# A gated recurrence and a low-rank mixer on one core: one more chunk's scaled k and q transposed by a DMA of SyncE, inside a new written-out order

## The chip, the core and the metric

The kernel runs on one core of a Trainium2 chip. A core has a tensor engine (PE, with its weight loads, PEld), a vector engine (VectorE, DVE in the profile), a scalar engine (ScalarE, ACT), GpSimd (POOL) and SyncE (SP), which here only issues DMA transfers. Each engine works through its own instructions strictly in the order in which they were issued; semaphores make it wait for the other engines. The metric is the device time of one execution in microseconds (us), lower is better.

## What is computed

Two operators, one after the other, in float32 (the kernel computes the products in bfloat16):

```python
# q, k, v, alpha: [batch 4, heads 8, rows 768, 48]
for t in range(S):
    state = alpha[:, :, t, :, None] * state + einsum('bhd,bhe->bhde', k[:, :, t], v[:, :, t])
    y[:, :, t] = einsum('bhd,bhde->bhe', q[:, :, t], state)
x = y.transpose(0, 2, 1, 3).reshape(4, 768, 384)
# U: [768, 32], V: [32, 768], w_ch1: [384, 1536], w_ch2: [1536, 384]
h = x.transpose(0, 2, 1) @ U @ V
u = x + h.transpose(0, 2, 1)
out = u + maximum(u @ w_ch1, 0) @ w_ch2
```

## The kernel before

**Recurrence.** The 768 rows of a batch are cut into six chunks of 128, so there are 24 chunks, named here (batch, chunk). Within a chunk, everything is expressed through the running sum of ln(alpha). One chunk goes through these steps (lines of `stage_pair`, which serves batches 0 and 1, then of `stage_gla`, which serves batches 2 and 3):

- four loads of 192 KB by SyncE (alpha, k, q, v; lines 347 and 354);
- ScalarE takes the logarithm of alpha into `lt` (377, 566), and v is copied to bfloat16 as `rv` (378, 567; by the helper `copy`, which issues on ScalarE at line 288, VectorE at 290 or GpSimd at 292);
- TensorE sums `lt` over the rows (386 and the lines behind it, 573 to 575);
- ScalarE takes three kinds of exponentials of that sum: `ai` and `aa`, with the whole chunk's width, and `tot`, a narrow one (400 to 402, 583 to 586);
- k times `ai` and q times `aa` become the two halves of `rkq`, on GpSimd or VectorE (408, 594);
- `rkq` is transposed into `kqt`. Mostly TensorE does it, in two groups of four products (436, 608), each followed by an eviction from PSUM on VectorE or ScalarE (`copy` again). For the chunks that stand in the tuple `QUEUE_T`, one transposing DMA transfer of SyncE does both halves at once (447, 620). Before the change `QUEUE_T` holds the six chunks of batch 3;
- scores: products of `kqt` with itself (467, 636), masked by VectorE into `pm` (478, 646);
- the state: a product of `rkq` with `rv` (501, 659), added to the earlier state (identity products at 493, or a sum `sm` at 530 and 686) and scaled by `tot` into `st` (516, 670);
- the result y: a product of `kqt` with the earlier state (in `stage_pair` that is `f_yi`, line 540; 698), plus products of `pm` with `rv` (550, 703), copied into `xb`.

`stage_pair` handles two spans of 128 rows for half of the heads in one chunk, with even and odd rows interleaved. `stage_gla` handles one span for all eight heads. `PAIRS` makes every chunk of batches 0 and 1 paired and none of batches 2 and 3.

**Mixer.** `stage_mix` multiplies `xb` with U (718 for batch 0, 728 for the others), then with V (749), and VectorE adds x into `ub` (759). Batch 0 goes another way, through products with the identity (769 to 772). The result is transposed into `uT`: for batches 2 and 3 (`QUEUE_U`) by three transposing DMA transfers of SyncE (783). `mlp1` is the first layer, 12 groups of three products for each half of a batch (829), each followed by a maximum with zero on ScalarE or VectorE (839, 841). `mlp2` is the second layer (858), the sum with u on VectorE (864), and the stores (867, 869). The weights come in 24 transfers of 192 KB (line 320) and are converted on GpSimd or ScalarE.

**The order.** None of this is issued where it stands. The functions only add operations to a list (`Plan.add`: engines that may do it with a planner's cost, the function, what it reads and writes, a `mode` letter for the way that the product uses the array). `Plan.run` then issues them in the order of `TABLE`, a string written out by hand. Each three characters are two for the number of the operation and one for its engine (P, A, D, G or S); `SLOTS` says which of its buffers each operation takes. Costs, modes and `kind` matter for a planner only: with a table they change nothing.

```python
            op = self.ops[code(x[0]) * len(CODE) + code(x[1])]
            for b in op.bufs:
                if b.slot is None:
                    place(b)
                ready.discard(b)
            op.fn({"P": "PE", "A": "ACT", "D": "DVE", "G": "POOL", "S": "SP"}[x[2]])
```

So `TABLE` sets the place of each operation in its engine's queue, and for SyncE the order of all transfers: loads, transposing transfers and stores share one queue. Buffers: 40 for loads and stores (`io`), four `kqt`, four `rkq`, five `rv`, three each of `aa`, `ai` and `lt`, eight banks of PSUM.

Decoded, the first transfers of the old order are (a for alpha, "1:" for batch 1, otherwise batch 0; the first has position 1): a0, a1, k0, v1, a2, a3, k1, q1, v0, q0, V, a4, k3, k2, a5, q2, k4, v2, **q3** (19th), v3, 1:a2, k5, q5, 1:a0, v4, q4, v5, 1:a1, 1:k0, 1:q0, 1:v0, U. Then the rest of batch 1's loads and the weights follow, mixed.

Of the kernel before, what the change touches and what calls it, by code (L numbers as in the profile page):

```python
# [20 lines left out]
HEAEeAGVPELPAqSECGEEPHFABiSEGDDfPEiPD9GEMPENDDgPDhDGYAHGAGXADiAEfPEgDD4PGWABlSEDGEFPEHAEhDD3PGqABmSAJPAKAAGPAHAD5PD6AD7A
EUGEjPEkDEIPEJDEKDGsPEmPEPPAmSGvAGZGGbPGdAAoSGaGElPEOPAkSGcPGeDEnPEpABjSBpSBqSEQPESAERAGUGGiPEoDBrSAySGjDGkDBnSGuAAuSAwS
GtAADGEqPGfPErPEsDB1SEzPEwPE8PHzAEtPE2PAsSE0PGlGE1DExPEyDA6SE5PEuPEvAE3PE4AE9PE+DE6PE7DH1PH4AANGA2SB0SAjAA4SGhDARGAPGE-P
FBPFCAFXPA0SFYAFDPFEDFADFbPFZPFaDHaAAfGAhGFrPHHGFTPFpPFqABsSFRPFSAH2AHcPFUDHeAHdAATGHfAFcAGxDGwGGyPH3AAZAAVGFVPGgDAXGFfP
FJPFFPFGAFsDB4SFKDGzPG1AHIDFtPFgAFuDBwSB+SBuSG0DFHPFIAHKPHMAHJPFdPFeAFWDAdGHLDBtSGrGG5PG6DHCGHQPIKAG7DG2PHNPFhPHRDHODFiA
G3DAbGFjPFnPFoABxSB8SHgGIMPHSDG4DHTDALGINAFkAArGFPPFNPFODB5SIOAHiPB6SHkDB3SBySB9SBzSG8GHhGFQAH6GFLPHjPHPDGmPIPAB2SBvSAnA
HVPHWPH8PHlDFlPH5GH7PH9DG9PFMAH+AFmAHXPHZDHYACASGnPGoDGpACDSG+PHbGHpPHqDHmPHoDCFSHnDH-PAlGApAIBDCESG-AHAAIQGGHPISPIUAHuP
IRGITPIVDF1PCMSACSHrGHvPIWPIADHwPH0GICPAvAHyAHxAAxAHsDCGSCBSCLSHUGIDDFvPIFPGNPIYDIEGIGPAtAILGIZPHtDIaDIHPIJDIbDIIDAzGF2P
KwAFwPA7AA1AIXDA5GA3GIcPGOPIdPKyPK0AK1AKzAIePIfACCSF3PGPPFxPIgDGQDFyDF4DCYSKHAKJPIhPGBPK3GIiDIjPKLAKNAGCPGIPInDKKALFALHP
K2AKMAKOGIlDImDIoPIkDIqDIrDGDPIpDKbAKdPKgAKeAKiGKPGKQPIsDLaAItPGJPGEDIuDIvPIwDLcPK5PIxPGKDIyDKSAK7AI1PI-PI2ALLALKAJAALdA  # L30
AIGKIGJLPJMAB7SLJALNDB-SLIAKcGI9PJbPKfAKjDJHPCUSKkPKhAI+AJcACOSCaSI5PJVPJWDJPPJQDKmALMDI7PJIDKRPI8AKTDI3PJDPJNPJXPJYAJZP
JEDK4GKXPKYDKlPJaAJTPLvAI6DLeALiGLgALfAJdPJOAKnAI4DK6PK8DJUDJFPJGDNcAIzPI0AKxGKrPKsDKtGJeDJJPJKANePNfANhAKUPKWDKoPK9PK-D
KpDKVDKqDNgANkGF7PJfPJgACQSJRPJSANiAF8PLOPLQDLxPK+DLyAN-AJhPJiALzALAPL0DF9PLBDLCDLDPLEAO1AOBPOEAKuPKvDF+DLPPLkPJ7PLhGL1G
L3PJ8PLRALGGL5DL2PL4DLjPNjGLbGOFAOCALVPLWDLXGCISJ9PLlAODAOHGKZPKaALSPLmDLnPLTDL6PJBPJCALoDLUDJjPLqPLrDLsGO3PJkPJpPLpDLtP
LYPJqPLwAO4AORAL7DL8DL9PO5ANtAJlPOTPAEGCHSCNSOGGJ+DLZDJmDLuAL+AL-PMADOWAJ1POUAOVANvPNxACJSCKSN1GCPSOAGNzAJoSMBPMDDMEDMCD
NuGNlSOXAMFDNwANyAJ2PKBPMGPMKDMJDMHDMIDJ3PJvPOjAOlPJwPKCPJrPN0DN6PJ4DJxPJyDNdANpPMLSNqDN7DMMSOnAOMPKDPKEDN8GONDMUPMgPMQP
MhDMSPMNSMmPMnAM2PMqPMrDMRAMaPMbDJsDMOPCTSOSGMWPMVAMPAMXAMoPOoAMpAMwPOpAMsPMePMYPMZDCRSCSSOYGCWSCVSMxAOmAM8PMTAMfANmPOIS
OJPM3DOLDMyPJ5SMuPMvAMtAOKDM6PM9AMzAOPPMcPMdANIPNnDNoDNrPNsAM7DCZSO6DOZGOaSObPOdDOcDOQDN2SN3PM4PM5AOePM+PMkPOOGOhPMiPMjA
M-PMlAO7GOrGN4DN5DN9PCXSOkAOqGOfDOgGOiDOsSOtPOuDO8SO9PO-DOwPOxDNJPO+DOvDCbSO2GNXPGSSGASGGSF5SN+AM0PNAPM1AF6SGRSOyGPAPPBD
OzPO0ANBDFzSKASJzSNKPNLDPCPPDDNSPGMSPEPPHDPFDPGDPIDPOSNTPNDPPJPPNDPKDNYPPLDPMDPPSNEPNNPNUPNVDNZPNOPNFPNPPPXPPYAPfPPVPPWA  # L40
# [12 lines left out]
"""


# [103 lines left out]
def kernel(  # L159
# [205 lines left out]
    def stage_pair(b, u, sprev, xb):  # L365
# [169 lines left out]
        yb = Buf(bank), Buf(bank)  # L535

        def f_yi(e, c):
            s = before[c]
            for a in range(2):
                nc.tensor.matmul(  # L540
                    yb[c]()[:, 2 * a * D : (2 * a + 2) * D], lhsT=qcol(a, c, slice(0, 128)), rhs=s[0]()[:, 2 * s[1] + a, :],
                    start=(a == 0), stop=False, skip_group_check=True,
                )
# [379 lines left out]
```

## Time and profile before

| | |
|---|---|
| time, median of three executions | 159.53 us (159.40 to 159.62) |
| the profiled execution's own time | 159.86 us |
| its span (first to last instruction) | 158.1 us |
| mean granted TensorE clock | 0.989 |
| data moved by DMA | 31.66 MB, mean 200 GB/s |
| DMA queue 1 (all transfers of the kernel) | 95,280 packets, 84.6% of 16 engines' span |
| VectorE, longest group | masks, line 646: 24 of 682 ns and line 478: 24 of 682 ns |
| ScalarE, longest group | relu, line 839: 65 of 504 ns |
| second layer, line 858 | 300 matmuls, 53.9 us of TensorE |
| first layer, line 829 | 288 matmuls, 51.9 us of TensorE |

How to read the rows that follow. A row of the strip has 40 digits, one for each fortieth of the span (3.95 us here), and a digit is the busy share in tenths. `out<-in` names what an instruction writes and reads, and `x4` is the number of instructions. "us A, B" after a bar are the total and the mean in ns; the number behind the second bar is the idle time of that engine just before, with what ended it. Times at the left of a row are from the start of the span.

### The profile page before, as it was taken

To read this page: it belongs to the slowest core of one execution; us is meant where nothing else is said; L and a number is where in the kernel's file an instruction comes from. 1 tells how busy PE (TensorE), PEld (TensorE's weight loads), DVE (VectorE), ACT (ScalarE), POOL (GpSimd) and SP (SyncE) were. 2 spreads that over 40 slices of the span, in tenths; PEclk is the share of its full clock that TensorE was granted. 3 is DMA by queue.
4 is the path that set the end of the run, shared out by engine and by line. 5 is a ranking of instruction groups with operands and counts; after the bars stand their busy time and mean duration, and the time that the engine had idled before them with its cause. 6 is when DMAs were issued, how large, how long until landed. Compare 5 with 4: busy or idle time off the path is not lost.

```text
span 158.1 us, 4788 instructions
## 1 busy us (share of the span) xinstructions
PE 146.3 (93%) x1864; PEld 99.4 (63%) x1864; DVE 105.2 (67%) x241; ACT 86.8 (55%) x225; POOL 63.6 (40%) x104
## 2 busy tenths in 40 slices
PE   0488699999999999999999999999999999999992
PEld 0376487756677666766767775655676566556671
DVE  5089578777989647937999978463998841602621
ACT  4486669758887475595977765038642103544100
POOL 8136696493996442504546534057313000000000
PEclk9999969999999999999999999999999999999999
DMA  4999899999999998998999986799997357343172
GB/s 119 280 278 307 219 287 248 316 330 294 266 311 282 267 189 160 215 197 169 191 202 184 216 170 133 115 181 206 209 145 183 92 101 205 114 154 77 50 249 100
DMA packets 95301, 31.66 MB, mean 200 GB/s; under 512 B 88976, under 2 KB 95248, under 8 KB 95280
## 3 DMA queue, kind: packets, MB, share of 16 engines
q1 hardware_dynamic: 95280, 31.37, 84.6%
q8 instruction: 14, 0.23, 0.6%
q14 instruction: 7, 0.06, 0.1%
HBM read 23.89 MB, written 4.72 MB: 181 GB/s over the span
## 4 chain that ended last, share of the span: by engine, by line
PE 86%; SPq 7%; DMA 3%; issue 1%; POOL 1%; DVE 0%
PE ps L858 30%; PE ps L829 30%; SPq L347 6%; DMA io<-in_q_dram 3%; PE ps L436 3%; PE ps L636 2%; PE ps L467 2%; PE ps L608 2%; PE ps L550 2%; PE ps L501 2%; PE ps L703 2%; PE ps L573 1%; PE ps L659 1%; PE ps L698 1%; PE ps L749 1%; PE ps L540 1%
## 5 line engine op out<-in xcount | busy, mean ns | idle before, releaser
L858 PE MATMUL ps<-w_sb,h1t 128*128 128x384 bf16 (+2 forms) x300 | 53.9, 320 | 0.0
L839 ACT ACTIVATE h1t<-ps 128x384 bf16<-128x384 f32 x65 | 30.9, 504 | 39.3 <-PE ps L829 39.1
L829 PE MATMUL ps<-uT,w_sb 128*128 128x384 bf16 x288 | 51.9, 326 | 0.0
L829 PEld LDWEIGHTS <-w_sb 128*128 128x128 bf16 x288 | 27.0, 98 | 16.6
L858 PEld LDWEIGHTS <-h1t 128*128 128x128 bf16 x300 | 27.3, 98 | 15.2
L841 DVE TENSOR_SCALAR h1t<-ps 128x384 bf16<-128x384 f32 x31 | 16.6, 553 | 17.8 <-PE ps L829 17.5
L292 POOL CAST rv<-io 128x384 bf16<-128x384 f32 x21 | 10.9, 527 | 16.4 <-DMA io<-in_v_dram 16.2
L478 DVE TENSOR_TENSOR pm<-ps,maskp 128x512 bf16<-128x512 f32 x24 | 15.7, 682 | 0.9 <-PE ps L467 0.9
L864 DVE TENSOR_TENSOR io<-ub,ps 128x384 f32<-128x384 bf16 (+2 forms) x19 | 9.8, 529 | 9.0 <-PE ps L858 9.0
L646 DVE TENSOR_TENSOR pm<-ps,maskc 128x512 bf16<-128x512 f32 x24 | 15.1, 682 | 1.0 <-PE ps L636 0.9
L594 POOL TENSOR_TENSOR rkq<-io,aa 128x384 bf16<-128x384 f32 x10 | 9.2, 915 | 7.7 <-DMA io<-in_q_dram 4.0
L436 PE MATMUL ps<-ident,rkq 128*128 128x128 bf16 x96 | 10.0, 242 | 2.1 <-POOL rkq L408 1.6
L288 ACT COPY kqt<-ps 128x512 bf16<-128x512 bf16 x16 | 9.7, 607 | 3.3 <-PE ps L436 2.4
L670 POOL TENSOR_TENSOR st<-sm,tot 128x384 bf16<-128x384 f32 x7 | 5.8, 830 | 14.1 <-DVE sm L686 14.1
L759 DVE TENSOR_TENSOR ub<-xb,ps 128x288 bf16<-128x288 bf16 x24 | 9.3, 449 | 2.8 <-PE ps L749 2.3
L386 PE MATMUL ps<-lt,upto 128*128 128x384 bf16 x12 | 4.8, 398 | 6.4 <-ACT lt L377 6.4
L594 POOL TENSOR_TENSOR rkq<-io,ai 128x384 bf16<-128x384 f32 x8 | 7.3, 915 | 7.6 <-ACT ai L583 3.9
L408 POOL TENSOR_TENSOR rkq<-io,ai 128x384 bf16<-128x384 f32 x10 | 9.1, 914 | 2.5 <-DMA io<-in_k_dram 1.3
L288 ACT CAST xb<-ps 128x192 bf16<-128x192 f32 (+1 forms) x23 | 7.8, 373 | 3.2 <-PE ps L703 2.0
L436 PEld LDWEIGHTS <-rkq 128*128 128x128 bf16 x96 | 7.1, 107 | 3.7 <-POOL rkq L408 2.3
L290 DVE COPY kqt<-ps 128x512 bf16<-128x512 bf16 x20 | 8.3, 418 | 0.8 <-PE ps L436 0.3
L377 ACT ACTIVATE lt<-io 128x384 bf16<-128x384 f32 x12 | 6.5, 538 | 4.1 <-DMA io<-in_alpha_dram 4.0
(116 smaller groups left out, 219.2 us busy)
## 6 DMA issues: line engine op xcount, KB each, us to landing
io<-in_alpha_dram SPq DMA_DIRECT2D x24, 192.0 KB, 4.0
io<-in_k_dram SPq DMA_DIRECT2D x24, 192.0 KB, 4.1
io<-in_v_dram SPq DMA_DIRECT2D x24, 192.0 KB, 4.0
io<-in_q_dram SPq DMA_DIRECT2D x24, 192.0 KB, 4.0
io<-in_moe_w_ch_dram SPq DMA_DIRECT2D x24, 192.0 KB, 4.4
out_dram<-io SPq DMA_DIRECT2D x24, 96.0 KB, 2.2
out_dram<-io SPq DMA_DIRECT2D x11, 192.0 KB, 2.0
out_dram<-io SPq DMA_DIRECT2D x1, 120.0 KB, 1.7
```

What stands on the lines that cost most here:

```text
L288: nc.scalar.copy(dst, src)
L292: nc.gpsimd.tensor_copy(dst, src)
L347: lambda e: nc.sync.dma_start(t().rearrange("p (h j) d -> p h (j d)", j=2), src[b, hs, sl, :].rearrange("h (p j) d -> p h (j d)", j=2)),
L436: nc.tensor.matmul(dst, lhsT=ring()[:, HP * j + 2 * a : HP * j + 2 * a + 2, :].rearrange("t h w -> t (h w)"), rhs=ident, start=True, stop= ...
L478: nc.vector.tensor_tensor(dst, s2, maskp.to_broadcast([C, 2, 2, C]), op=ALU.mult)
L594: eng.tensor_tensor(dst()[:, :, 0:D], a(), x(), op=ALU.mult)
L646: nc.vector.tensor_tensor(pm()[:, :, par, :], s2, maskc.to_broadcast([C, HP, C]), op=ALU.mult)
L829: nc.tensor.matmul(hb()[:, 0:TW], lhsT=w1_sb[:, ct, jt * 128 : (jt + 1) * 128], rhs=u_half(uT, ct, tt, b in QUEUE_U), start=(ct == 0), sto ...
L839: nc.scalar.activation(dst, hb()[:, 0:TW], AF.Relu)
L841: nc.vector.tensor_scalar_max(dst, hb()[:, 0:TW], 0.0)
L858: nc.tensor.matmul(hb()[:, 0 : hi - lo], lhsT=h1()[:, jt, c * C : (c + 1) * C], rhs=w2_sb[:, jt, lo:hi], start=(jt == 0 and not low), stop ...
L864: P.add({"DVE": 468}, lambda e, hb=hb, lo=lo, hi=hi: nc.vector.tensor_tensor(flat(ou)[:, lo:hi], (xb if low else ub)()[:, c, lo:hi], hb()[ ...
```

## The change

Three edits. First, `QUEUE_T` also takes (2, 5), the last chunk of the third batch: its two groups of transposing products and two evictions go, and a transposing transfer of SyncE comes. Second, `f_yi` in `stage_pair` gets a loop over the two interleaved halves for a paired chunk that stands in `QUEUE_T`; for a paired chunk that does not, the loop does what stood there before. No paired chunk is in `QUEUE_T`. Third, `TABLE` and `SLOTS` are replaced, from 1060 entries to 1057 (four fewer, one more), so most operations have another place than before. Matmuls fall from 1864 to 1856.

```diff
 TABLE = """
-A8SCcABASCzAA9SBDSC1PC3ACePBESDKABISC0GBBSC2AC5DCfACiDDjABCSC6DDMPDOACgAChADPAC7PC9DA-SCdGA+SCjDABSDlPDmAAFGDoADnACkPCmD
...
+BCSA8SCcACePBASCzAC1PC3ABISBDSBBSBESCfAChADjADlPA9SC6GC8PDKAC2ADMPA-SCgAC4ADmABMSCiGC5DC7PC9DC0ADCPDDDBKSD8ACdGCrPCsDC+A
...
-    QUEUE_T = tuple((3, c) for c in range(6))
+    QUEUE_T = tuple((3, c) for c in range(6))+((2,5),)
...
         def f_yi(e, c):
             s = before[c]
             for a in range(2):
-                nc.tensor.matmul(
-                    yb[c]()[:, 2 * a * D : (2 * a + 2) * D], lhsT=qcol(a, c, slice(0, 128)), rhs=s[0]()[:, 2 * s[1] + a, :],
-                    start=(a == 0), stop=False, skip_group_check=True,
-                )
+                for j in range(2):
+                    if queued:
+                        rs = slice(64 * j, 64 * j + 64)
+                        lhs = qT()[:, 2 * j + a, 64 * c : 64 * c + 64]
+                    elif j == 0:
+                        rs = slice(0, 128)
+                        lhs = qT()[:, 2 * a + c, :]
+                    else:
+                        continue
+                    nc.tensor.matmul(
+                        yb[c]()[rs, 2 * a * D : (2 * a + 2) * D], lhsT=lhs, rhs=s[0]()[:, 2 * s[1] + a, :],
+                        start=(a == 0), stop=False, skip_group_check=True,
+                    )
...
-                P.add({"PE": mm(2 * D, 2 * D)}, lambda e, c=c: f_yi(e, c), r=[qT, before[c]], w=[yb[c]])
+                P.add({"PE": mm(2 * D, 2 * D)}, lambda e, c=c: f_yi(e, c), r=[qT, before[c]], w=[yb[c]], mode="K" if queued else "F")
```

Decoded, the new table differs from the old one most at the start and in SyncE's queue:

- The first transfers now are: q1, a0, a1, a3, v1, k1, a2, k0, v0, a4, q3, q0, k3, a5, q2, V, k2, v2, **v3** (19th), 1:a0, k5, k4, q5, q4, v4, 1:a2, 1:a1, a weight (group 3, row block 1), v5, 1:q0, 1:k0, 1:v0, U. The same loads, but for one weight, make up both lists.
- ScalarE's copy of v3 (`rv` of chunk 3) stands, in its queue, behind `aa` of chunk 4 and ahead of the narrow exponentials of chunk 3, of `ai` and `aa` of chunk 5, of two more groups of narrow ones, and of the logarithm for batch 1's first chunk.
- The new transposing transfer of (2, 5) is SyncE's 106th entry, behind the alphas of chunks 5 and 4 of batch 3 and ahead of the alpha of its chunk 2.
- In batch 3, T standing for a chunk's transposing transfer and uT for the three of batch 2's mixed result, the old queue has a0 and q0 of batch 3 as its 96th and 99th entries and runs, from the 106th on: a4, q2, q5, a3, a1, v0, k2, k1, q1, v2, a store, T0, uT, uT, uT, v3, k3, q3, q4, k4, T2, a store, k5, T3, T1, v4, T4, T5, v5. The new one runs, from the 106th on: T of (2, 5), a2, q2, k1, q1, q5, a3, v2, k2, k3, v1, uT, uT, q0, uT, T2, q3, T0, v3, k5, k4, q4, T3, T1, v4, T4, T5, stores, v5.
- TensorE's order behind batch 0's mixing stays near the old one, operation by operation, and its last groups are the same.

More of the change, by code (lines that the diff above doesn't have):

```diff
@@ L21 @@
[L21 to L40, printed above, removed]
@@ new lines @@
+BSSDrPDtDEVPBOSBPSBcSBYSAgSBTSBWSBVSDoADLGCuDBXSCoPCpDDGPDZPAASAOSBkSAMSBfSAQSAiSEWAEZGEXAAWSBaSDyPDzPD0DDHPDIDAeSEYADPA
+DaPDbDGTAAUSASSDJABmSDSPDUABdSGVPGXABjSCqDBZSCvPD1PD2DBbSDcPDdDAaSBeSBoSBgSEbPEdAAcSDWPDXDGWAGYAAJPAKAEaGEcPDvPEeADePBlS
+DfPHBACwPCyADYDDgPAYSBiSAmSDwDDxDCxAEfPEhDEgDDhAAGPAHADiAECGEEPEGDGqAEDGEFPEHAHDPHGAD4PD3PELPHFAD9GEiPEMPENDHEAD5PD6AD7A
+BhSBrSAoSAqSEUGEjPEIPGsPGvAGuAEOPGtAEkDEmPEPPElPAkSEJDEKDGaGGcPGeDBqSAwSGZGGbPBpSEnPEoDEQPEpDBnSGUGGiPGjDGkDADGEqPGdAGfP
+ESAERAErPE2PEwPE5PEtPE8PEsDExPEyDEzPEuPEvDE9PAsSANGAPGA4SHzAE0PE1AE3PE4AE6PE7DE+DH1PH4AH3AH2AAjAARGFDPE-PFBPAfAFEAAySAuS
@@ new lines @@
+AhGB3SFZPGgDA2SFaDGxGAVGGzPA6SFVPFTPGhDFRPFSDA0SFWDATABwSFADFXPFYAG1AAXGFHPHHDFIAGrAGlGGwGFtPFuDFfPFJPFUAHJPHIGFrPFpPFqA
+HCAFhPFiAAbAFgAHLDFCDIKAB0SFsDFKDHaAFFPFGDG5PG6DHQPB1SBsSGyPG0DG7DFbPFdPFeAHRDFcAHKPHMDH6GH8PIMPIPAINAG8GB8SBxSBtSBzSCAS
+HSGAdGBvSB2SH5DHTDBuSH+AHcPHeAHfAG2PG4DB4SHNPHPDHODG3DAZGFLPFMDFnPFNPHdAHVPIOAFOAFlPFmAFjPFkAG9PH7PH9DFPPHhGHjPFoAFQAByS
+HbGHlAHgGApGHiPArGHkDHWPGmPHXPHYDHZAG+PHAAG-DAxAGnPGoAGpAHpPHqDHrDHmPHnDAnGH-PIADHoDIBDAlGF1PGHPILGFvPHsDB6SB+SIRGITPIVD
+HvPA5AHuPIQGISPALGAIGIUDHwPHxAIZPHyDHtDIaDH0GICPHUGIDDAvGGNPB-SIWPIcPCCSIXDAtAAzAIEDIbDF2PCBSGOPB7SB5SFwPIdPIFPA3GIYDIGP
@@ new lines @@
+IePIfAIHPCISIIDCESA7GA1GF3PF4DB9SFxPKbAKdPIgAIJAIhPGPPKwAKyPFyDGQDIiAIjPIkDKeAKiGK0AK2AKHAIlDK1AGIPKzAInDGBPImDKJPIoPIsD
+IrDKgAGCPKKAKOGItPKLAIuAKkPGDPIpDIqDIvPGEDKMAGJPIxPACSIwDI9PJBPIyDIzPI0DKhAJCAKNAI7PI8DJbPJXPLaAKIGKXPLvALFAGKDJYDCDSJPP
+JQDKmAKYDJdPLHPJcALLALKAJeAJTPK4GLcPJUDKfAK6PKPGI-PJADLeALfALJAJJPJKDLdALIAI+AJLPJMDK8DJNPJODKQPKjGLxPKlPK3GK5PK7DLyAKRP
+KTDLgAKSALzAKnAKcGKrPKsDJRPJSAI1PI2DKUPK9PKWDK+DKoPKqDF7PL0GI3PLiGK-DJZPJfPI4ANqAKVDKpDJVPLNGJWDJFPJhPJgAJDPKtDJGDJEDNZA
+LMGKxGLAPCFSCHSLkPL1GCYSCUSL2SJaACMSLDPLEALbAI5PLhGLjPLPPI6ACOSLmDKuPKvAJiDLlALRDLBDLOPLQDF8PKZPNbPNeANdAKaDLnPLSPLoDLTD
@@ new lines @@
+J7PLUDLpDF9PF+DLGGLVPJjPLCGLWDLXGLqPLrDJ8PLYPLZAOgAN8ALwAL3PL5DL4DCJSCKSCaSCQSJHPJkPLtPLuAJIAN+PN-AJ9PJ+DCPSLsGL6PAEGCNS
+L7ACRSCLSOAAOCAJlPJmDOBAOEDNfAL8PL9AJpPNcAL+PMBDMCDMADOOAL-DNaAMISJqPNsPKBPMDPMEDMHDJvPOQPORAN9AKCPOiPMGDMFDMJSNgGNmPNuA
+KDPKEDJ1PCGSNvAOSANtANxGJwPJ2PJxPJyDOyAOlAOmAJ3PNyDNrGN3PJ4DJrPMPPOkAOjAMLPMNPJsDMMAMKSMODNnDMQDOUAMRPMVPMWDMpPMqAMtPMuD
+MfPMrPM1PMgDN4DMjPM2DMsAMSANwAODGOFSOGPCSSNhGMkANiSNjPMbPMcAM3POHDO0PCTSOWGMvPOIDOVGNlDM4DN5GOMPONDCZSCVSOPGOTAO2AMzPOJP
+OKDMhPM0DNkDMlPMmACWSOoDMnPMoDOnGMwDMdPMeDMZPO1AO3GO4GMXPMTPMUDOXSNoPOYPMiAMaAOaDNzSMYAN0PN1DOZDM7PObPOLGOcDN2DOdGM5PM8P
@@ new lines @@
+NFPM9PM+DCXSOhANpAOtPOuDOvGN6POpSOqPOsDO5SO6POrDO8DJzSO7DNGPCbSOzGGRSM-SN7DOePOfDNUPMxPOwPOxAO9PO+ANHPMyDM6DNIDO-PNPPPAA
+PBPPFDPDDPEDPCDGGSJoSGASNQPNAPKGSJnSPGPGMSGLSF6SKASNVPPJDPHDPLSNRPPKDPIDNKPPMSNBPNLPPNSNCPNMPNWPNXDJ5SJuSNYSPePNDDPQPPSP
+PRAPkPPUPPVDPlAPfDPaPPbDPTDJ6SNJSPYPPZDGFSF0SPyPPuPPOPPPDPzDPqPPmPPnAPrAPoPPpAQDPP2PP3ANNDP6PPgPPcPPdAPWPPXDPwPPsPPvAP4P
+P7AP5DF-SPiPP+PPtAPhAQcPQXPP-PQEPQIPPjANSDKFSGSSNTSF5SNOSJ-SPxDJ0SNESQFPP0PP1DP8PP9DQAPQBDQCSQdPQGDQHSFzSJtSQJPQePQfDQgS
+QKPQYPQLDQMSQNPQZPQaDQOPQSPQPPQTPQbSQQDQRSQUPQVDQWS
@@ L50 @@
-ADCBDACACBHCFfGDEBEBAFDCGBAeCBDCBAFGBHDCCBFABCAFGBACAHAAChalAFBADBCEBiBAmCDGHBFBADCHCBEGFBGEnKDCCDBBBFAADFCAEHBFHCCDEFDB
-HCAFHEBJkCDHGCEACFBAEBCBHBGCADGABFABHGDCBEDCFOBBBCAHBDEDABALCAFADBIREAFHDBGCACEBHDGTDBEBHFDEBHEFYHCEFBUADCEAHCAHcMCHPDEX
-NBjFe
+ABAACBBADEFGAACCHADABEIBBCJBFAAGHAKBBABBDFLMNAOCCADAGBABCCFPDCHDBQRCSTUVGDWXYZabcdDDeFGBHBfghijkCAAlmACCFAnBAADABCDDAECG
+HFFIEJLHAKBDCADGCAHBMEBGONPADCBABFBCGHABACAEEBCRQSTADGFCBCBAEHAVCDBDUWDXYBGFDABDAHECGFAABbcAEBCAGBHAZdeCAhCFfEDGgjCCABDG
+CEFBACGBBaCDFHABAmBEBGDAFACEDBklnCHBAFBEAHBCBDBDFGCACDCHAGEFDBDGiACAEDBCBAGACEHCFCBABEDAIJCEBFHCGACEBCLHFGMADAKONEHFGRST
@@ L53 @@
+AGHBEPVBFADHAABCACCCFAHEDCBDDBBEAQBHDCABHCFADABCWUHDCBEDFCCAHACBBBABFCGABEFCDBABHBGCFADBCAHEBGACDADCEBCBFAAADcXHYdAhACEE
+CFbCADAHBECCFADCABHfCBFBBDDACBAAAGCZgjaBCDClBCGnAFBAECCBABBHGDBABCFCEGDHBEADHADAkGHDBBBDCBCCiBABGHmAACAGHDBGHBDBBGCDCAFH
+BDKDBABGBJIECFEAAHNAGEFCCHCCDGBCAAFBHEDBCCBeGADABABGEADFHBMDDEGHFRAHADFGCCABCFGADTFOBGBCEABCEFAGBFCLGDABCAEBGADEdBHhUbaC
+XBc
 """
```

11 lines of the change are left out of this document (1 added, 10 removed).

## The prediction

> **What bounds the kernel now.** I read the page first, then busy time by stretches, then who waits for whom on TensorE.
>
> ```profile
> span 158.1 us, 4788 instructions
> PE 146.3 (93%) x1864; PEld 99.4 (63%) x1864; DVE 105.2 (67%) x241; ACT 86.8 (55%) x225; POOL 63.6 (40%) x104
> PE   0488699999999999999999999999999999999992
> PEclk9999969999999999999999999999999999999999
> ```
>
> TensorE is full from the sixth slice (20 us) to the end; only the start, and one slice of lowered clock in it, is not. The stretches and TensorE's own waits say the same in numbers:
>
> ```profile
> 16.00:24.00 8.00, 6.79 (x150) 5.53 (x154) 5.20 (x13) 5.35 (x15) 6.21 (x9) 0.79 1.00 254
> 24.00:32.00 8.00, 7.93 (x184) 5.96 (x184) 6.76 (x16) 6.71 (x21) 4.57 (x9) 1.00 1.03 283
> ...
> PE ps L386 <- ACT lt L377: 6.4, 3, 4.6
> PE ps L436 <- POOL rkq L408: 1.6, 2, 1.2
> PE ps L436 <- DVE rkq L408: 0.4, 1, 0.4
> ```
>
> After each stretch and its length stand TensorE, weight load, VectorE, ScalarE and GpSimd (busy us, instructions), the clock, the DMA share. All of TensorE's waits sum to 8.4 us, and the last that matters ends here:
>
> ```profile
> 12.22 5.21 DMA io<-in_q_dram
> 17.50 0.91 POOL L408 TENSOR_TENSOR rkq<-io,aa 128x384 bf16<-128x384 f32 x1 [1.54 <-DMA io<-in_q_dram]
> 18.46 0.40 PE L436 MATMUL ps<-ident,rkq 128*128 128x128 bf16 x4 [1.20 <-POOL rkq L408]
> 20.77 0.52 PE L386 MATMUL ps<-lt,upto 128*128 128x384 bf16 x1
> 22.44 0.33 PE L386 MATMUL ps<-lt,upto 128*128 128x384 bf16 x1
> 28.25 0.28 PE ps L718 x4
> ```
>
> The 19th transfer, q of chunk 3, lands 5.21 us after its issue, at 17.43 (the median of its kind is 4.0); GpSimd scales it, and TensorE restarts at 18.46 after 1.20 us. Then its clock is low for a while: the same product takes 0.52 us at 20.77 and 0.33 at 22.44. From 18.46 on it always has work, so I split the time: the way to the first product of batch 0's mixing (28.25), which the loads set; the TensorE work behind it, which adds up one to one; and a tail behind the last matmul, the same in both.
>
> **The change part by part.** *The transposes of batch 2, chunk 5.* Eight go from TensorE, two evictions from ScalarE or VectorE, and one transposing transfer is added to SyncE's queue.
>
> ```profile
> 69.52 0.22 PE ps L608 x4
> 77.82 0.78 PE ps L636 x24
> 87.28 0.81 PE ps L636 x24
> 110.15 0.55 PE ps L636 x16
> 114.59 0.59 PE ps L829 x3
> 116.01 0.49 PE ps L829 x3
> ```
>
> Four transposes cost 0.22 us, so 0.45 goes. The evictions are hidden behind TensorE's full queue; I cost them at nothing. If that cover were gone, each would be worth the 0.4 to 0.6 us of a copy.
>
> *Switches between array modes.* A product that uses part of the array next to one that uses all of it costs extra: 24 score products take 0.78 and 16 take 0.55, so eight take 0.23, and 0.55 less 0.46 leaves 0.09 for leaving the mode; a first-layer group right behind one takes 0.59, not 0.49, for entering. So 0.1 us for a switch. Decoded, the old order has 62 and the new one 67: three more ahead of the first mixing product, two more behind it. Behind it that makes -0.45 + 0.20 = **-0.25 us**.
>
> *The rewritten product with the earlier state* (`f_yi`) costs nothing: only paired chunks call it, they lie in batches 0 and 1, and no such chunk is in QUEUE_T. It issues the same two matmuls.
>
> *The start.* Most early loads have one size and land one after another, so I give the n-th transfer of the new queue the landing of the n-th of the old. The new order needs as its 19th the v of chunk 3, where the old has that q.
>
> ```profile
> L288 ACT CAST rv<-io 128x384 bf16<-128x384 f32 x3 | 1.6, 518 | 0.0
> L583 ACT ACTIVATE ai<-ps 128x384 bf16<-128x384 f32 x12 | 6.0, 499 | 0.5 <-PE ps L573 0.4
> 19.38 0.53 ACT L377 ACTIVATE lt<-io 128x384 bf16<-128x384 f32 x1
> 21.73 0.34 PE ps L493 x2
> 26.77 0.19 PE ps L540 x4
> 47.66 0.71 PE ps L550 x48
> ```
>
> Landing at 17.43, copied by ScalarE in 0.52 where the old order scaled on GpSimd in 0.91, it lets TensorE restart at about 18.05, 0.4 earlier. But less is done by then: the old order has also run one chunk's scores (some 0.25, near the 0.23 above, and a switch), half a state product (0.1) and two value products (0.24 each, from 0.71 for three), less two identity products (0.34 for two at the low clock, so 0.1 each at the full one) and two switches that the new one has run; that is about 0.55. The three switches more add 0.3. So 0.85 - 0.4 = 0.45 us later at the mixing.
>
> Then the wait itself: the copy of v stands in ScalarE's queue ahead of the exponentials of chunk 5, of two pairs of small ones, and of the logarithm for batch 1's first chunk. These start at 18.0: about 0.2 + 2 x 0.45 + 0.53, so the logarithm is done at 19.65. TensorE has four groups until then, some 0.9 us, to 18.95, and idles 0.7 more. Half of that is given back if the clock is low there anyway, as it was from about 19.0 to 22.4 in the old run: 0.35. Bounds: 0 (the old order, with the same queue, waited nowhere between 18.46 and 28.25) to 0.7; with 0.25 to 0.35 in the middle the mixing is **0.7 us later**.
>
> *A rule on the clock.* The low clock follows a gap of 1.20 us. The Trainium skill, "TensorE: Matmul & The Clock Gate", "Why this matters for your kernels", asks only that no gap exceed about 3 us; by that rule neither kernel would slow down, which this trace contradicts (0.52 against 0.33 us behind a gap of 1.20). By the rule the new start would come out as in the first rival below.
>
> *SyncE's queue later.* The new transfer is the 106th. Its neighbours and the transposing ones:
>
> ```profile
> 82.36 0.92 SPq L354 DMA_DIRECT2D io<-in_alpha_dram  x1
> 94.80 1.34 SPq L620 DMA_TRANSPOSE kqt<-rkq  x1
> 96.90 4.90 SPq L783 DMA_TRANSPOSE uT<-ub  x3
> DMA to landing us min/median/max: 3.1/3.8/5.3
> io<-in_q_dram SPq DMA_DIRECT2D x24, 192.0 KB, 4.0
> L594 POOL TENSOR_TENSOR rkq<-io,aa 128x384 bf16<-128x384 f32 x10 | 9.2, 915 | 7.7 <-DMA io<-in_q_dram 4.0 <-ACT aa L584 3.1 <-DMA kqt<-rkq 0.7
> 94.98 0.24 PE ps L749 x12
> 96.65 0.24 PE ps L749 x12
> ```
>
> It should be issued near 82.4 and land 3.1 to 5.3 us later, 85.5 to 87.7. The scores that read it are TensorE's work at about 88.3 (the third group of the row at 87.28, with 0.3 us more work ahead of it and the later start), so 0.6 to 2.8 us are left: I take nothing. It holds the queue for 1.34 us in place of 0.92, so the next load, the alpha of batch 3's chunk 2, is 0.4 later; its logarithm (0.53) is due near 89, with over one us to spare. If the transfer waited for GpSimd's scaling, all behind it would be late by as much; k and q of that chunk are the 94th and 93rd transfers, a dozen places of some 0.9 us sooner, so I take nothing here either.
>
> **Sum.** +0.7 - 0.25 = +0.45 us. The profiled execution took 159.86 us (span 158.1 and 1.76 around it), the median of three runs is 159.53; by the same difference that becomes **160.0 us**, or 160.3 for a profiled one.
>
> **The rivals.** *First: the start stays warm, and it is faster.* If the 19th transfer lands at its turn, about 0.6 us after the 18th and not 1.9, near 16.1, TensorE has hardly a gap (by VectorE's evictions and state products behind the 15th transfer, its last product before that wait ends near 16.5, a rough estimate) and the clock stays up. Then loads bind:
>
> ```profile
> 19.76 0.55 SPq L347 DMA_DIRECT2D io<-in_k_dram  x1
> 28.18 0.61 SPq L320 DMA_DIRECT2D io<-in_moe_w_ch_dram  x1
> io<-in_moe_w_ch_dram SPq DMA_DIRECT2D x24, 192.0 KB, 4.4
> ```
>
> v of chunk 5 becomes the 29th transfer (issue 19.76, landing near 24.0), and five GpSimd instructions behind it (two scalings of 0.92, three conversions at the 0.5 of a copy) allow the mixing at 27.4. The weight that is now 42nd (28.18 + 4.4, some 0.3 more as the DMA engines are full, and 0.5 to convert) is needed 5.5 us of work behind the mixing, which holds that to 27.9. That is 0.3 to 0.4 earlier than 28.25: -0.3 - 0.25, or **159.0 us**. For it: 5.21 us is far from the median of 4.0. Against it: if what delays that transfer belongs to that time and not to it, whichever is the 19th meets it.
>
> *Second: a transposing transfer of batch 3 comes too late, and it is slower still.* In the old order q of batch 3's first chunk loads as the 99th transfer, some 30 us before use. In the new one it stands behind the first two transfers that transpose batch 2's mixed result. These follow the products at 94.98 and 96.65 by about 1.9 us; the new order reaches these products some 1.4 us earlier, so the second is issued near 97.2 and the load, behind its 1.6 us in the queue (4.90 for three), near 98.8. It lands at 102.8, GpSimd scales it by 103.7, the transfer lands 3.8 us later, at 107.5, and the scores want it at 108.0 (110.15 in the old order, 2.7 us less work ahead, 0.5 later start). Half a us is left; at 5.3 us to landing TensorE waits 1.0, one to one to the end, with VectorE's masks and the next two transposing transfers queued behind it. It decides from 4.3 us on. Price: 160.0 + 1.0 = **161.0 us**. For it: every step is serial, and two of its transfers must keep to their medians. Against it: the median of six such transfers is in time.
>
> *Third: nothing shows.* The start comes out as before (bounds: 0 for the wait, the earlier restart offsetting what is undone) and -0.25 remains: **159.3 us**.
>
> **How the numbers follow.** Less than 0.2% (0.32 us) can't be told from no change here. The forecast gets 0.40, the first rival 0.29, the second 0.22, the third 0.09. The forecast's own range is 159.5 to 160.5 (the bounds of the start), so of its 0.40 I count 0.28 as slower, 0.10 as same and 0.02 as faster; the first rival gives 0.27 to faster and 0.02 to same; the second 0.21 to slower and 0.01 to same; the third 0.06 to same and 0.03 to faster. Sums: faster 0.32, same 0.19, slower 0.49. The range takes in the first rival and most of the second: 158.9 to 161.3.
>
> **What would show it.** Right: TensorE's wait near 16.5 to 18 ends on ScalarE's copy of v (`rv`), a second, shorter one on ScalarE's `lt`; a low-clock slice near 20 us; the first mixing product at 28.5 to 29.3; no gap from there to the last matmul; eight matmuls fewer at the transposes' line. Wrong: a mixing product ahead of 28.2, full clock in the sixth slice, or TensorE waiting for a `kqt` transfer near 88 or 108 us. The sum is also wrong if loads land well off their turn, since all of the start hangs on that one assumption.

## The result, and the profile after

The changed kernel takes **160.18 us** (median of 21 runs, 159.26 to 161.24), the kernel before 159.35 (21 runs, 158.39 to 161.18). By these medians it is slower by 0.83 us. The ratio is 1.006, 95% interval 1.0038 to 1.0082. (The ratios here and below leave out the few runs that are more than 1.5% above the fastest of the same kernel; the medians take in all runs.) The forecast was 160.0 and +0.45 against its own 159.53. So the sign and the rough size came out, but not by the way that was forecast, as the rows show.

The page of the changed kernel, the same lines as before:

```profile
span 159.4 us, 4775 instructions
PE 146.6 (92%) x1856; PEld 97.6 (61%) x1856; DVE 111.7 (70%) x249; ACT 81.0 (51%) x216; POOL 65.8 (41%) x103
PE   0489897979999999999999999999999999999992
PEclk9999999999999999999999999999999999999999
```

The row has TensorE's clock full in every slice: the low slice near 20 us that the prediction named is not there, and full clock in the sixth slice is one of its own signs of being wrong. There are two weaker slices instead, the seventh and the ninth (24 to 28 and 32 to 36 us), where the kernel before was full. The stretches of the changed kernel:

```profile
16.00:24.00 8.00, 7.48 (x197) 5.41 (x191) 6.99 (x15) 7.57 (x25) 5.45 (x8) 1.00 0.99 264
24.00:32.00 8.00, 7.11 (x160) 5.26 (x156) 6.07 (x15) 5.06 (x18) 4.49 (x8) 1.00 0.88 229
32.00:48.00 16.00, 14.65 (x158) 9.23 (x157) 12.68 (x26) 11.48 (x30) 9.62 (x15) 1.00 1.04 299
```

and the one of the kernel before that the prediction did not show:

```profile
32.00:48.00 16.00, 16.00 (x207) 10.92 (x206) 12.87 (x28) 12.30 (x32) 13.11 (x22) 1.00 1.05 296
```

From 16 to 24 us the changed kernel does more (7.48 us busy at full clock, against 6.79 at 0.79). It then idles 0.89 us from 24 to 32 and 1.35 us from 32 to 48, where the kernel before idles 0.07 and nothing. TensorE's timeline of the changed kernel, the rows with a wait (start, duration, and in brackets the idle time before it and what ended it), with its first mixing product:

```profile
26.94 0.40 PE L436 MATMUL ps<-ident,rkq 128*128 128x128 bf16 x4 [0.89 <-POOL rkq L408]
27.95 0.35 PE L727 MATMUL ps<-xb,ue_sb 128*32 128x384 bf16 x4
...
34.29 0.40 PE L436 MATMUL ps<-ident,rkq 128*128 128x128 bf16 x4 [0.89 <-POOL rkq L408]
...
38.99 0.40 PE L436 MATMUL ps<-ident,rkq 128*128 128x128 bf16 x4 [0.27 <-DVE rkq L408]
45.17 1.15 PE L838 MATMUL ps<-uT,w_sb 128*128 128x384 bf16 x6 [0.18 <-POOL w_sb L292]
```

The first mixing product stands at 27.95, not later but 0.23 earlier than before (28.18 in this view). That is a second of the prediction's signs of being wrong ("a mixing product ahead of 28.2"). What follows it is longer: the last matmul ends at 156.43 against 154.95. The waits are those for the transposes of batch 1's chunks 0, 1 and 2 and for a weight. The chain of waits of the changed kernel names the one at 33.4 us whole:

```profile
27.61 1.12 SPq L320
28.73 0.04 issue
28.77 4.39 DMA io<-in_q_dram
...
33.32 0.92 POOL rkq L408
34.25 0.05 issue
34.29 0.40 PE ps L436 x4
```

q of batch 1's chunk 1 is the 41st entry of SyncE's queue, issued at 28.77 and landed 4.39 us later; GpSimd scales it in 0.92 us, and TensorE, which has this transpose next in its order, waits 0.89 us for it.

One caution: this execution took 161.24 us, the slowest of the 21. The experiments therefore begin with further executions of the same two kernels.

### The profile page after: what moved, and what is told of

Same layout as the page of the kernel before. It is cut to its first block, busy times and chain, and to the rows that moved or that the text cites. A ratio compares the mean times of both kernels' runs of the same rounds, so it can differ in the third digit from the quotient of the medians.

```text
span 159.4 us, 4775 instructions
## 1 busy us (share of the span) xinstructions
PE 146.6 (92%) x1856; PEld 97.6 (61%) x1856; DVE 111.7 (70%) x249; ACT 81.0 (51%) x216; POOL 65.8 (41%) x103
## 4 chain that ended last, share of the span: by engine, by line
PE 71%; SPq 16%; DVE 5%; DMA 3%; issue 2%; POOL 2%; POOLq 0%
PE ps L867 30%; PE ps L838 25%; SPq L347 12%; SPq L320 3%; DMA io<-in_q_dram 3%; DVE pm L655 2%; PE ps L645 2%; PE ps L436 2%; PE ps L712 1%; PE ps L617 1%; PE ps L582 1%; PE ps L707 1%; PE ps L668 1%; PE ps L559 1%; DVE h1t L850 1%
## 5 line engine op out<-in xcount | busy, mean ns | idle before, releaser
L867 PE MATMUL ps<-w_sb,h1t 128*128 128x384 bf16 (+2 forms) x300 | 53.2, 320 | 0.0
L838 PE MATMUL ps<-uT,w_sb 128*128 128x384 bf16 x288 | 50.8, 326 | 0.2 <-POOL w_sb L292 0.2
L850 DVE TENSOR_SCALAR h1t<-ps 128x384 bf16<-128x384 f32 x50 | 25.9, 552 | 14.7 <-PE ps L838 13.6
L848 ACT ACTIVATE h1t<-ps 128x384 bf16<-128x384 f32 x46 | 21.8, 494 | 24.8 <-PE ps L838 24.4
L603 POOL TENSOR_TENSOR rkq<-io,ai 128x384 bf16<-128x384 f32 x12 | 11.0, 920 | 17.5 <-ACT ai L592 12.5
L288 ACT CAST xb<-ps 128x192 bf16<-128x192 f32 (+1 forms) x25 | 8.7, 391 | 17.4 <-PE ps L712 12.0
L408 POOL TENSOR_TENSOR rkq<-io,aa 128x384 bf16<-128x384 f32 x11 | 10.0, 914 | 8.6 <-ACT aa L401 4.3
L603 POOL TENSOR_TENSOR rkq<-io,aa 128x384 bf16<-128x384 f32 x9 | 8.3, 937 | 8.9 <-DMA io<-in_q_dram 5.3
L408 POOL TENSOR_TENSOR rkq<-io,ai 128x384 bf16<-128x384 f32 x9 | 8.3, 927 | 4.8 <-DMA io<-in_k_dram 2.2
L288 ACT COPY kqt<-ps 128x512 bf16<-128x512 bf16 x15 | 8.8, 596 | 1.5 <-issue 1.1
L292 POOL CAST w_sb<-io 128x384 bf16<-128x384 f32 x16 | 7.9, 527 | 3.9 <-DMA io<-in_moe_w_ch_dram 3.8
L436 PEld LDWEIGHTS <-rkq 128*128 128x128 bf16 x96 | 6.2, 101 | 5.3 <-POOL rkq L408 3.2
```

The source lines that it names most:

```text
L288: nc.scalar.copy(dst, src)
L408: eng.tensor_tensor(jh(dst()[:, :, 0:D]), raw(a), jh(x()), op=ALU.mult)
L436: nc.tensor.matmul(dst, lhsT=ring()[:, HP * j + 2 * a : HP * j + 2 * a + 2, :].rearrange("t h w -> t (h w)"), rhs=ident, start=True, stop= ...
L603: eng.tensor_tensor(dst()[:, :, 0:D], a(), x(), op=ALU.mult)
L838: nc.tensor.matmul(hb()[:, 0:TW], lhsT=w1_sb[:, ct, jt * 128 : (jt + 1) * 128], rhs=u_half(uT, ct, tt, b in QUEUE_U), start=(ct == 0), sto ...
L848: nc.scalar.activation(dst, hb()[:, 0:TW], AF.Relu)
```

## The experiments

Two numbers of each profile carry the readings: the start of the first mixing product of batch 0 (all that comes ahead of it is "the start"), and TensorE's idle time between 24 and 46 us (22.00 less its busy time in that stretch). The last column is the end of the last matmul.

| kernel | runs | median us | ratio to the kernel before, 95% | first mixing | idle 24 to 46 | last matmul |
|---|---|---|---|---|---|---|
| before | 21 | 159.35 | | 28.18 | 0.07 | 154.95 |
| before, second execution | 1 | 159.06 | | 26.88 | 0.68 | 154.15 |
| before, third execution | 1 | 159.90 | | 27.26 | 0.33 | 154.97 |
| changed | 21 | 160.18 | 1.006 [1.0038, 1.0082] | 27.95 | 2.24 | 156.43 |
| changed, second execution | 1 | 159.97 | | 27.02 | 1.66 | 155.17 |
| changed, q of (1, 1) earlier | 12 | 159.51 | 1.0023 [0.9993, 1.0054] | 27.50 | 1.35 | 154.42 |
| changed, transposes of (1, 1) later | 12 | 159.99 | 1.0062 [1.0033, 1.0092] | 27.11 | 1.76 | 155.17 |
| before, with the transposing transfer alone | 12 | 159.78 | 1.0029 [0.9997, 1.0060] | 26.69 | 0.13 | 154.11 |
| changed, 16 products more | 12 | 160.06 | 1.0051 [1.0020, 1.0083] | 26.48 | 1.36 | 155.05 |
| changed, three loads later | 12 | 158.69 | 0.9979 [0.9945, 1.0013] | 26.31 | 0.81 | 154.45 |
| the same, measured again | 12 | 159.47 | 1.0025 [0.9989, 1.0060] | 26.45 | 0.36 | 153.43 |
| three loads later, U earlier | 12 | 159.40 | 1.0026 [0.9997, 1.0056] | 27.98 | 0.96 | 154.60 |

The kernel before had medians of 159.35, 159.09, 159.04 and 158.82 us in the four groups of runs.

**The changed kernel once more.** Expected:

> The changed kernel once more, to see which of TensorE's waits belong to the order and which to the one profiled execution (161.24 us, the slowest of 21). Theory W (the order puts transposes of batch 1 ahead of what the load queue can deliver): TensorE again waits at the transposes of batch 1's chunks 0, 1 and 2 between 25 and 40 us, 1.0 to 2.0 us in sum, and the first mixing product is again at 27.5 to 28.5. Rival N (those waits belong to one bad execution): less than 0.5 us of waits between 25 and 46 us, and the loss against the kernel before lies ahead of the mixing.

Measured: 159.97 us, near the median. Its timeline has the same waits at the same places, smaller:

```profile
26.01 0.40 PE L436 MATMUL ps<-ident,rkq 128*128 128x128 bf16 x4 [0.64 <-POOL rkq L408]
31.27 1.80 PE L838 MATMUL ps<-uT,w_sb 128*128 128x384 bf16 x10 [0.20 <-POOL w_sb L292]
33.37 0.40 PE L436 MATMUL ps<-ident,rkq 128*128 128x128 bf16 x4 [0.30 <-POOL rkq L408]
37.95 0.40 PE L436 MATMUL ps<-ident,rkq 128*128 128x128 bf16 x4 [0.29 <-DVE rkq L408]
44.13 1.64 PE L838 MATMUL ps<-uT,w_sb 128*128 128x384 bf16 x9 [0.18 <-POOL w_sb L292]
```

That is 1.61 us of waits. So they come with the order, and their size varies with the execution. The first mixing product came at 27.02, half a us ahead of the range given.

**The kernel before, twice more.** Expected:

> The kernel before once more, to see what of its start belongs to the order and what to one execution. If the late 19th transfer (5.2 us), the wait of 1.20 us behind it and the low clock from 19.0 to 22.4 us belong to the order, they are here again, with the first mixing product at 28.0 to 28.5. If they belong to the one profiled execution, the wait is shorter, no clock below 1.00 is granted behind it, and the first mixing product stands at 26.5 to 27.3. The stretch from the first mixing product to the last matmul is 126.7 us in either case, within 0.3.

> The kernel before a third time, with the same question and the same numbers as the second: a spread of its first mixing product over 1 us or more would say that the start of both kernels varies by more from one execution to the next than the change moved it.

Measured: first mixing at 26.88 and 27.26. The same stretches of the second execution:

```profile
16.00:24.00 8.00, 7.32 (x204) 5.62 (x203) 6.77 (x17) 6.96 (x20) 6.28 (x9) 1.00 0.95 243
24.00:32.00 8.00, 7.32 (x143) 5.10 (x132) 5.94 (x13) 5.39 (x17) 4.57 (x9) 1.00 0.87 251
32.00:48.00 16.00, 16.00 (x236) 11.03 (x238) 13.17 (x28) 12.71 (x33) 13.63 (x22) 1.00 1.08 316
```

The clock is 1.00 from 16 to 24 us, where the first execution had 0.79. The 19th transfer, q of chunk 3, took 4.48 and 3.82 us to land in these two, against 5.21, and no wait of TensorE behind 12 us ahead of the mixing is longer than 0.74 us. The wait of 1.20 us and the low clock, on which the prediction's picture of the start rested, thus belong to some executions and not to the order as such. How often shows in the mean granted clock of the runs: half the clock for 3.41 us of 158 makes it 0.989, and 8 of the 75 runs of the kernel before in the three later groups have 0.989 or less, as has 1 of the 21 of the changed kernel. From 32 to 48 us TensorE is full, as in the first execution. The other expectation failed: from the first mixing product to the last matmul it is 126.77 us in the first execution, but 127.27 and 127.71 in these two, which start earlier and wait for weights behind it (0.78 us at 54.8 in the third, 0.29 at 30.8 in the second).

**One load earlier.** SyncE's queue, places 37 to 41 (v2 and q1 are loads of batch 1, the others weights):

```diff
-v2, w, w, w, q1
+q1, w, w, w, v2
```

> The changed kernel with two loads exchanged in SyncE's queue: q of batch 1's chunk 1 becomes the 37th transfer and v of its chunk 2 (not read before 40 us) the 41st. Theory W: that q lands near 30.5 in place of 33.2, TensorE's 0.89 us wait at 33.4 is gone, and 0.4 to 0.9 us of it reach the end: about 159.4, ratio to the kernel before 1.001. Rival L (the loads as a whole are late, whichever comes first): the wait moves to the next transposes at 38.7 or to the weights at 45, and the time stays at 160.2, ratio 1.005.

Measured: 159.51, ratio 1.0023. The waits left in its timeline between 24 and 46 us:

```profile
25.62 0.40 PE L436 MATMUL ps<-ident,rkq 128*128 128x128 bf16 x4 [0.58 <-POOL rkq L408]
26.49 0.40 PE L436 MATMUL ps<-ident,rkq 128*128 128x128 bf16 x4 [0.47 <-POOL rkq L408]
43.39 1.64 PE L838 MATMUL ps<-uT,w_sb 128*128 128x384 bf16 x9 [0.18 <-POOL w_sb L292]
```

The wait at 33.4 is gone and none took its place; from the first mixing product to the last matmul it is 126.92 us, where the changed kernel had 128.48 and 128.15. The intervals of the two ratios still overlap, so the gain of 0.4% is likely rather than certain; the vanished wait is certain for this profile.

**TensorE's transposes later.** The loads as in the changed kernel; on TensorE:

```diff
-transposes of scaled q of (1, 1); first layer of batch 0, groups 11, 10, 9
+first layer of batch 0, groups 11, 10, 9; transposes of scaled q of (1, 1)
```

> The changed kernel with its loads as they are, but on TensorE the transposes of the scaled q of batch 1's chunk 1 stand behind three first-layer groups (1.47 us) that stood right behind them. Theory W: the wait of 0.89 us at 33.4 is gone, since the scaling is done at 34.24 and the transposes now come at about 34.9; the result is not read before 44 us; the end is 0.4 to 0.9 earlier, about 159.4, ratio 1.001. Rival L: the first-layer groups that come sooner wait for their own weights instead (group 11 needs the weights that land at 34.05), so that less than 0.3 us is gained, ratio 1.004 or more.

Measured: 159.99, ratio 1.0062, no gain. The wait moved, as the rival said:

```profile
33.55 1.64 PE L838 MATMUL ps<-uT,w_sb 128*128 128x384 bf16 x9 [0.99 <-ACT w_sb L288]
```

Group 11 now waits 0.99 us for its own weight, the 42nd entry of the queue. So this exchange on TensorE does not mend it: two transfers side by side are both late for it.

**The transposing transfer alone, in the old order.**

```diff
-    QUEUE_T = tuple((3, c) for c in range(6))
+    QUEUE_T = tuple((3, c) for c in range(6))+((2,5),)
 TensorE
-scores (2, 3), (2, 4), (2, 5); four groups
+scores (2, 3), (2, 4); four groups; scores (2, 5)
 SyncE
-alpha of (3, 3)
+transposing transfer of (2, 5); alpha of (3, 3)
```

> The kernel before with only the named edit: the scaled k and q of batch 2's last chunk go through one transposing transfer of SyncE, put ahead of the load of alpha of batch 3's chunk 3; eight matmuls and two evictions go; that chunk's scores stand behind four later TensorE groups so that the transfer can land. By the prediction's term: -0.45 us, ratio 0.997, with no wait of TensorE near 89. Rival: the transfer waits for GpSimd's scaling at 84.3, holds the queue, and batch 3's loads or TensorE at 89 wait for it: ratio 1.000 or more.

Measured: 159.78, ratio 1.0029 with an interval that holds 1: the -0.45 us did not show in the time. It does show in place. From batch 1's first product with V to the scores of (2, 3), where the edit does no more than take out the eight transposes, first the second execution of the kernel before, then this kernel:

```profile
60.40 0.31 PE L749 MATMUL ps<-utx,ve_sb 32*128 32x96 bf16 x12
...
86.59 0.88 PE L636 MATMUL ps<-kqt 48*128 48x128 bf16 x24
```

```profile
59.71 0.31 PE L749 MATMUL ps<-utx,ve_sb 32*128 32x96 bf16 x12
...
85.46 0.66 PE L636 MATMUL ps<-kqt 48*128 48x128 bf16 x16
```

That is 26.19 us (26.19 and 26.28 in the other two executions) against 25.75: -0.44. But the edit has a cost that the expectation left out: it tears the scores of (2, 5) from their row, which makes 64 switches between array modes in place of 62, and from the start of the scores to the second layer behind them (88.88 there, 88.04 here) the same products take 2.58 in place of 2.29 us, +0.29. There was no wait near 89, but one further on:

```profile
101.50 1.80 PE L829 MATMUL ps<-uT,w_sb 128*128 128x384 bf16 x10 [0.64 <-DMA uT<-ub]
```

TensorE reached batch 2's first layer some 1.4 us sooner than in the first execution of the kernel before, and the second transposing transfer of the mixed result, issued at 97.06, took 4.4 us in place of 3.2 (issued at 98.51 there). Whether the added transfer in the queue or chance made it slower, one profile does not say. So the run confirms the term of the transposes where it arises, and the split scores and the wait of 0.64 us take it back before the end.

**The saved work put back.** In the changed kernel, the score products of (2, 5) made three times:

```diff
-            for p in range(HP):
+            for p in list(range(HP)) * (3 if (b, c) == (2, 5) else 1):
```

> The changed kernel with the score products of batch 2's last chunk made three times in place of once (the second and third time write the same numbers): 16 products more of the kind of which eight take 0.23 us, at the place where the eight transposes were saved. If TensorE's work there adds one to one, as the prediction has it, the first product of batch 3's mixing and the end come 0.45 to 0.5 us later relative to batch 0's mixing than in the changed kernel, ratio 1.009 to the kernel before. Rival: the work saved there is taken up by waits behind it (for the transposing transfers of SyncE's queue), so that 16 products more cost less than 0.2 us, ratio 1.006.

Measured: 160.06, ratio 1.0051, not 1.009: its start was the earliest of the changed order (26.48), and 0.46 us lies within the intervals. The profile tells it apart behind the start. From batch 1's first product with V to the last matmul, first this kernel and then the second execution of the changed one:

```profile
60.17 0.31 PE L758 MATMUL ps<-utx,ve_sb 32*128 32x96 bf16 x12
...
153.79 1.26 PE L867 MATMUL ps<-w_sb,h1t 128*128 128x144 bf16 x15
```

```profile
60.75 0.31 PE L758 MATMUL ps<-utx,ve_sb 32*128 32x96 bf16 x12
...
153.74 1.43 PE L867 MATMUL ps<-w_sb,h1t 128*128 128x240 bf16 x17
```

That is 155.05 - 60.17 = 94.88 against 155.17 - 60.75 = 94.42: +0.46 for 16 products (two times the 0.23 of eight). One profile is enough for this difference, since the stretch hardly varies: in the seven other profiles of the changed order, those with loads moved among them, it is 94.42 to 94.44 once a wait of 0.15 us in the first is taken off. TensorE's work there counts one to one.

**Three loads later.** SyncE's queue of the changed kernel, all else as it was:

```diff
-28: weight (group 3, block 1);  37: v of (1, 2);  47: v of (1, 3)
+37: weight (group 3, block 1);  48: v of (1, 2);  56: v of (1, 3)
```

> The changed kernel with three transfers that nobody reads soon moved back in SyncE's queue, and nothing else: the weight of group 3, row block 1 from the 28th to the 37th place, v of batch 1's chunk 2 from the 37th to the 48th, v of its chunk 3 from the 47th to the 56th. So q, k and v of batch 1's chunk 0 come one place sooner (0.6 us), k of its chunk 1 two places, k of its chunk 2 and the weights between one place. Theory W (TensorE's waits from 25 to 46 us are single transfers that stand too far back): the waits there fall from 1.6 to 2.2 us to less than 1.0, the end comes 0.6 to 1.0 us sooner than with the changed kernel, ratio to the kernel before 0.999 to 1.002. Rival L (the loads as a whole bind, so any order of them costs the same): another wait takes their place, ratio 1.005.

> The changed kernel with the three later transfers once more, for a narrower interval: 158.4 to 159.0, ratio to the kernel before 0.996 to 1.000 if the gain of the first measurement (0.9979) is real and the version beats both kernels; 1.003 or more if that was luck.

Measured: 158.69, ratio 0.9979, and in the second measurement 159.47, ratio 1.0025. TensorE's stretch from 24 to 46 us in this kernel's second measurement, then in the changed kernel's first execution:

```profile
24.00:46.00 22.00, 21.64 (x305) 14.87 (x304) 18.29 (x40) 16.81 (x46) 13.98 (x25) 1.00 1.04 304
```

```profile
24.00:46.00 22.00, 19.76 (x299) 13.13 (x295) 16.92 (x37) 15.14 (x43) 12.10 (x20) 1.00 0.97 268
```

The idle time fell from 2.24 (1.66 in the second execution) to 0.36 (0.81 in the first measurement), by moving back three transfers that nobody reads soon. Part of it lies at the start: the wait for the transposes of batch 1's chunk 0, ahead of the mixing (0.89 and 0.64 us before), is gone, and the first mixing product comes at 26.31 and 26.45. From there to the last matmul it is 128.14 us in the first measurement's profile, no shorter than before, and 126.98 in the second's. In the time, no loss against the kernel before is left that can be told from nothing: the two ratios lie on either side of 1, though the interval of the second still overlaps that of the changed kernel (1.0038 to 1.0082). That it beats the kernel before is not shown: 1.0025 lies between the two cases that were set out, nearer to the second (luck).

**U earlier as well.**

```diff
-32: the two transfers of U
+26: the two transfers of U
```

> The same kernel with the two transfers of U (the op of SyncE whose issue takes 1.5 us, with another 1.4 us for the issue behind it) moved from the 32nd to the 26th place. In the profile of the kernel with three later transfers the landings have a gap from 25.56 to 28.86 us behind them. If that gap comes from the issue standing still while few transfers are outstanding, it shrinks by 0.5 to 1.5 us when U goes earlier, the weights of group 0 land near 28.5 in place of 29.8, TensorE's waits between 29 and 33 go, and the time is 0.3 to 0.8 us lower: about 158.2, ratio 0.994. If the stall only moves (chunk 0 of batch 1 and the last chunks of batch 0 come later by it), the first mixing product is 0.5 to 1 us later and the time is 158.7 or more.

Measured: 159.40, against 159.47 for the same kernel without this edit in the same group of runs. The first mixing product came at 27.98, 1.5 us later than without the edit, as the second case has it: the stall seems to have moved, and nothing was gained.

## Why the prediction was right, and where it was not

The total held: +0.83 us where +0.45 was forecast, inside the forecast's own range. **Both large terms were wrong, and their errors, of opposite sign, cancelled in good part. That the total held is luck.**

*The start (+0.7).* It is not later. With the old order the first mixing product stands at 28.18, 26.88, 27.26 and 26.69 (the last in the kernel with the transfer alone, whose start is the old one), 27.25 on average; with the new one at 27.95, 27.02, 27.50, 27.11 and 26.48, 27.21 on average (the kernels with three loads moved are left out of it). The step that failed is "I give the n-th transfer of the new queue the landing of the n-th of the old". The changed kernel's transfers that were being issued from 11.80 to 12.20 us and from 12.88 to 13.50, with their time to landing as the last number:

```profile
io<-in_v_dram SPq DMA_DIRECT2D x1, 192.0 KB, 4.0
...
io<-in_k_dram SPq DMA_DIRECT2D x1, 192.0 KB, 5.2
```

The 19th took 4.0 us; the slow one was now the 21st, a k of chunk 5 that GpSimd had no time for before 18.2 anyway. The prediction itself named this weakness in its first rival ("5.21 us is far from the median of 4.0") and gave it 0.29. The copy of v, the second wait for ScalarE's logarithm and the low clock, all built on that landing, did not come about: from 16 to 24 us the changed kernel idles 0.52 us, at clock 1.00.

*The clock.* In the first execution of the kernel before, the low stretch has sharp edges; the row ahead of it is the stretch of the same length just before:

```profile
15.60:19.01 3.41, 1.82 (x61) 1.34 (x62) 2.06 (x5) 2.16 (x7) 1.87 (x4) 1.00 0.85 209
19.01:22.42 3.41, 3.41 (x53) 2.83 (x53) 2.05 (x6) 2.12 (x5) 3.41 (x6) 0.50 1.09 281
```

Half the clock was granted for 3.41 us, right behind 3.41 us in which TensorE was busy for 1.82, or 53%. In the changed kernel the emptiest such stretch behind its start keeps the clock at 1.00:

```profile
24.00:27.40 3.40, 2.51 (x71) 1.89 (x68) 2.42 (x6) 2.32 (x9) 2.34 (x4) 1.00 0.76 172
```

There it was busy for 2.51, or 74%. Whether the busy share of a stretch decides or its longest gap (1.20 us, against at most 0.99 behind 16 us in the profiles without a fall) these profiles cannot tell; one such fall was profiled, and no threshold was measured. (The row's full clock in its first slices is not to be relied on: the same product, line 386, takes 0.53 us at 12.89 and 0.34 at 15.31 in the changed kernel, and 0.53 at 9.43 and 0.32 at 12.99 in the kernel before. So TensorE is slower in both until some 12 to 15 us.) The Trainium skill, "TensorE: Matmul & The Clock Gate", "What's actually happening", has a free-running window of 3413 ns, which the length of the low stretch fits; that a window must be idle for the fall, as its table has it, does not agree with the 53%.

*Behind the mixing (-0.25).* Measured from the first mixing product to the last matmul: 128.48 and 128.15 us with the new order, 126.77, 127.27 and 127.71 with the old, so about 1 us more. Most of it is idle time: 1.51 and 1.02 us of these stretches with the new order, 0.01, 0.29 and 0.80 with the old. The term of the transposes, -0.45, was sized rightly: taken out alone they gave 0.44, and as many us put back cost 0.46. The two switches more (+0.20) fit, by an estimate: from batch 1's first product with V to the last matmul it is 93.75 to 93.93 us in the three executions with the old order and 94.43 with the new, which has there four wide products more (0.16 each), three narrow ones more (0.04 each) and the eight transposes less; that explains 0.34, and 0.16 to 0.34 is left for the switches. The step that failed stood earlier, in the reading of the old profile: "From 18.46 on it always has work", which was carried over to the new order. I followed the loads of batch 0 and the late part of SyncE's queue, and priced at nothing the loads between, the 28th to the 56th. Among them v of (1, 2) and v of (1, 3) had moved from the 51st and 62nd place to the 37th and 47th, and the weight of group 3, block 1, from the 37th to the 28th, ahead of what TensorE's new order needs first. That these cause the waits is shown: exchanging one pair removes one wait, moving three back removes most of the idle time. That they are the whole loss is likely (ratios 0.9979 and 1.0025 with them moved) but within the noise.

*The new transfer.* Right. SyncE issued it at 84.26 (82.4 forecast); its time to landing, here the changed kernel's transfers issued from 84.2 to 84.3, is within the 3.1 to 5.3 given:

```profile
kqt<-rkq SPq DMA_TRANSPOSE x1, 4.0
```

It landed at 88.2, and the scores stand at 89.67 with no wait.

*The rivals.* The first (a warm start) was what happened up to the mixing, with 27.95 measured for its 27.9. That the figures agree is chance: the second execution had 27.02, and a late k of (1, 0) held the first there and not a weight; its 159.0 failed for the same reason as the forecast. The second (batch 3's transposing transfer too late) did not happen: no wait of TensorE behind 82.6 us, and the seven such transfers took 3.2 to 4.8 us. The one of batch 3's first chunk took 3.4 and landed at 108.75, for scores that begin at 109.03 with another chunk's, so it was as close as the rival had it. The third had the start right and missed the waits. `f_yi` was not measured by itself; its new branch is never taken.

## What to carry to other kernels

When an order is replaced, follow every transfer of the new queue to its first reader, in the middle too, and not only those near the named edit: here the named edit gave its 0.45 us, and loads that nobody reads for some 10 us took about 1 us back by standing ahead of those that are read next. A wait in one profile may be that of one execution: look at two or three before a sum is built on it. Where the queue of loads bound, moving the reader did not help here (the next reader waited), while moving back loads that are read late cost nothing that showed and took the waits away.

## What was not expected of the hardware

The slow loads have a companion in time. A 16 KB packet of the queue called "instruction" starts in each of the stretches 15.58 to 15.62 and 23.38 to 23.45 us of the changed kernel (first number: packets):

```profile
q8 instruction: 1, 0.02, 166.6%
...
q8 instruction: 1, 0.02, 83.1%
```

The loads that took 5.2 us (the 21st, landed at 18.11) and 5.6 us (k of (1, 0), 20.26 to 25.84, the cause of the wait at 26.05) were both outstanding then. In the kernel before, one starts between 14.95 and 15.05:

```profile
q8 instruction: 1, 0.02, 59.2%
```

with the 5.21 us load of the prediction outstanding. The landings pause from 15.51 to 17.43 there, from 16.36 to 18.11 and from 23.91 to 25.84 in the changed kernel, where the landings around them come some 0.6 us apart. In the twelve profiles together, 48 such packets start between 13.9 and 36.8 us, and for 47 of them a pause of over 1 us in the landings spans that moment or begins within 1.5 us behind it. Pauses of that length also come without a packet (from 41.08 to 42.81 in the changed kernel), and that the packets make the pause was not tested. That the pause belongs to a time and not to a place in the queue does show: with the old order's start it delays the 19th, the 18th, the 20th and the 18th transfer in four profiles.
